# Sparse attention with a gated convolution: last output in 64-row transfers, x without padding, a convolution by shifted ranges

## The chip, the cores and the metric

One of the eight cores of a Trainium2 chip runs the whole program. The metric is the time of one execution in device microseconds (us), lower is better. The host only lays the arrays out.

## The reference

Eight batches of 576 tokens, eight heads of 64 columns. Four heads attend locally, four with a stride of 32; their outputs side by side are x (576 x 512 per batch). Then a causal convolution of five taps per column makes a gate, and a matrix product makes a value:

```python
x = np.ascontiguousarray(attn_out.transpose(0, 2, 1, 3)).reshape(B, S, H * D)
xp = np.concatenate([np.zeros((B, K - 1, D), dtype=np.float32), x], axis=1)
gate_pre = np.zeros((B, S, D), dtype=np.float32)
for k in range(K):
    gate_pre += conv_w[k][None, None, :] * xp[:, k:k + S, :]
gate = 1.0 / (1.0 + np.exp(-gate_pre))
val = x @ w_val
return (gate * val @ w_out).astype(np.float32)
```

## The kernel before

**Tiles.** Every batch is done for its first 512 tokens (MAIN); the last 64 tokens (REST) of all eight batches are gathered in the tile xe and done at the end as a ninth "batch" of 8 x 64 tokens (`b == B`). x lies transposed, columns on the partitions: tiles of 128 partitions x 4 column tiles (index ct or e) x 512 tokens. For float32 accuracy each operand of a product is split in two parts of type fp32r, high and low, and a product is three: high by high, high by low weight, low by high. The parts of x are xhi and xlo, two buffers each, taken in turn by the batches; the parts of the gated value are ghi and glo; the weights are wv and wo, two tiles each.

**Where the operands lie.** Lines 128 to 130 make the parts of x with 16 more elements ahead of each row of 512 (PADX): rows of 528 elements, 2112 bytes apart, and the 512 tokens begin 64 bytes into each. The rows of ghi, glo, wv and wo are 512 elements, 2048 bytes apart, and these tiles follow one another without a gap (lines 132 to 137), so all of their rows begin at the same distance from a multiple of 2048. xe is allocated between the parts of x and ghi.

**Value (line 457) and projection (line 473).** For each batch four chains of twelve matmuls of 512 columns make the value: stationary wv, moving xhi or xlo. VectorE multiplies the result by the gate (GV), ScalarE makes the high part, GpSimd the low part. Four more chains of twelve make 128 rows of output each: stationary ghi or glo, moving wo. In the ninth batch xhi[1] and xlo[1] take the place of ghi and glo (line 455).

**Gate (line 430).** ScalarE and VectorE do the five taps, except for the first two column tiles of batch 0 (CONV, line 541). There TensorE does them: GpSimd builds diagonal matrices in ghi and glo (line 438), and 15 matmuls of 512 columns, five taps by three products, read x at starts 4 to 0 tokens early (line 443). The four elements ahead of each row that they reach are zeroed once by two ScalarE copies (line 516).

**Output (line 496).** ScalarE scales a chain's result into one of two buffers of 128 x 512 (osb, a ring of two) and SyncE's queue (SP) issues one transfer of 128 rows, 256 KB. In the ninth batch the 128 partitions of a chunk are 64 rows of one batch and 64 rows of the next, 576 rows apart; line 495 describes them as one transfer by the destination pattern `[[S * DM, 2], [DM, REST], [1, DM]]`. In the very last chunk, m = 3, ScalarE does one half of the columns and VectorE the other.

**Order.** Each instruction is a step with a number, in the order in which the code adds it; SEQUENCE (line 543) is the order in which the steps are issued, written out by hand, with `f` tokens for filler matmuls. Each engine works its own steps in that order. It ends with "1482 1485 1483 1484 1491 1486 1487 1488 1492 1493 1494 1489 1490": matmul chains of chunks 0, 1, 3, 2 of the ninth batch, and the scaling and the transfer of chunk 3 ahead of those of chunk 2. Chunk 3 takes the output buffer that chunk 1 has had, chunk 2 that of chunk 0. Early in the sequence step 102 is VectorE's subtraction that makes the first third of xlo of batch 0; the GpSimd step before it in the sequence is 61 (low part of wv2) and the one behind it 143 (first scaled probabilities, PS, of the strided heads).

Of the kernel before, what the change touches and what calls it, by code (L numbers as in the profile page):

```python
# [8 lines left out]
F32 = mybir.dt.float32  # L9
F32R = mybir.dt.float32r  # L10
# [11 lines left out]
KC = 5  # L22
PADK = KC - 1
PADX = 16
# [34 lines left out]
def tile_sparse_attention_moe(  # L59
# [22 lines left out]
    def tiles(n, shape, name, dtype=F32, space=None):  # L82
        return [(space or pool).tile(shape, dtype, name=f"{name}{i}") for i in range(n)]
# [42 lines left out]
    vSs = pool.tile([P, 8, 256], F32, name="vSs")  # L126
    xss = tiles(2, [P, 4, PADK + S], "xs")
    xhp = tiles(2, [P, 4, PADX + MAIN], "xhi", F32R)
    xlp = tiles(2, [P, 4, PADX + MAIN], "xlo", F32R)
    xhi, xlo = [t[:, :, PADX:] for t in xhp], [t[:, :, PADX:] for t in xlp]  # L130
    xe = pool.tile([P, 4, B, PADK + REST], F32, name="xe")
# [7 lines left out]
    cws = tiles(2, [P, 4, KC], "cws", F32R)  # L139
    cw64 = pool.tile([P, 4, KC, 2], U32, name="cw64")  # L140
# [167 lines left out]
    def attend_local(b):  # L308
# [3 lines left out]
        for u in range(3):  # L312
# [65 lines left out]
            dve(group, V.tensor_tensor, out=lo, in0=mine, in1=hi.bitcast(F32), op=ALU.subtract)  # L378

# [52 lines left out]
    def gate(b):  # L432
        xs = xss[b % 2]
        for e in range(4):
            gt, group = gates[e][:, :], f"G{b}.{e}"
            if (b, e) in CONV:

                dg = diags[e]
                wide = [P, KC, P]
                for h in range(2):  # L440
                    gps(group, G.affine_select, out=dg[:, h, :, :], in_=cws[h][:, e, :, None].to_broadcast(wide),
                        pattern=[[0, KC], [-1, P]], compare_op=ALU.is_equal, fill=0.0, base=0, channel_multiplier=1)
                cp = m_ps.next()[:, :]
                terms = [(h, xx, k) for k in range(KC)
                         for h, xx in ((0, xhp[b % 2]), (1, xhp[b % 2]), (0, xlp[b % 2]))]
                pe(group, [mm(cp, dg[:, h, k, :], xx[:, e, PADX - PADK + k:PADX - PADK + k + MAIN], i == 0, i == len(terms) - 1)
                           for i, (h, xx, k) in enumerate(terms)])
                act(group, A.activation, out=gt, in_=cp, func=AF.Tanh, scale=0.5)
                continue
# [29 lines left out]
    def project(b):  # L479

        for m in range(4):
# [16 lines left out]
            if b < B:  # L498
                dst = out[b * S + m * P:b * S + m * P + P, :]
            else:  # L500
                first = out[2 * m * S + MAIN:2 * m * S + MAIN + 1, :]
                dst = bass.AP(tensor=first.tensor, offset=first.offset, ap=[[S * DM, 2], [DM, REST], [1, DM]])
            plan.add("sp", group, [(nc.sync.dma_start, dict(out=dst, in_=osb))])
# [12 lines left out]
    for t in (xhp[0], xlp[0]):  # L516
        act("zero xs", A.copy, out=t[:, 0:2, PADX - PADK:PADX], in_=none[:, :, None].to_broadcast([P, 2, PADK]))
# [26 lines left out]
f0x6 f0x4 f0x3 f0x6 44 0 1 32 73 71 37 22 74 72 2 18 3 75 7 46 45 8 5 38 9 33 35 47 181 10 17 11 23 76 48 4 12 21 6 50  # L544
29 20 27 13 56 24 34 81 25 14 49 87 16 31 78 15 39 88 80 103 26 89 62 90 104 f0x1 79 40 91 41 105 119 77 92 187 120
183 51 257 93 121 94 260 52 19 95 57 259 106 96 f0x3 f0x1 f0x1 53 182 258 58 107 54 184 30 55 108 185 122 97 109 28
111 64 63 110 59 99 42 136 123 205 65 98 137 158 f0x3 43 138 186 139 124 140 112 f0x2 60 141 125 113 36 100 114 126
188 127 159 f0x1 101 61 115 142 66 84 102 128 160 143 193 116 129 161 131 210 83 189 130 70 85 132 209 190 82 289 133
144 86 134 67 145 117 272 f0x1 f0x1 191 264 135 118 162 199 192 211 146 273 266 163 69 265 194 164 274 263 147 195 149
275 148 206 196 276 154 277 165 150 68 166 290 306 151 278 197 291 280 421 207 167 155 279 156 423 152 198 307 171 169  # L550
308 200 157 292 153 170 201 168 309 293 176 294 172 202 177 323 310 267 295 178 296 281 173 422 179 174 225 297 324
219 420 180 175 325 282 261 283 220 326 284 226 213 262 311 208 221 212 298 214 327 345 f1x1 301 312 203 222 313 429
# [89 lines left out]
```

## Time and profile before

| | us |
|---|---|
| runs, median of 3 (331.93 to 332.74) | 332.56 |
| the profiled execution, its own time | 329.11 |
| span of the profiled execution, first to last instruction | 327.3 |
| TensorE (PE) busy | 297.6 (91%) |
| VectorE (DVE) busy | 229.0 (70%) |
| ScalarE (ACT) busy | 217.5 (66%) |
| GpSimd (POOL) busy | 149.4 (46%) |

Line 54 is the line of the helper that issues all steps, so most rows carry it; they are told apart by their tiles, written out<-in. PEld is TensorE's loading of stationary operands, which overlaps PE. Matmuls are pipelined, so the distance from one start to the next says more than the duration of one. SPq is the issue of transfers by SyncE. Square brackets at the end of a timeline row give the idle time of the engine before it and what ended it; "x2" means that neighbours of one kind were merged.

### The profile page before, as it was taken

The numbers are of one execution on the slowest core, as the hardware profiler recorded it, in microseconds if no ns is written. First come the engines' busy times: TensorE is split into PE (matmuls) and PEld (weight loads), VectorE is DVE, ScalarE is ACT, GpSimd is POOL, SyncE is SP. The second block draws the span as 40 slices with busy tenths as digits, with TensorE's granted clock in tenths as the row PEclk, the third lists the DMA queues.
The fourth block names the chain that finished last, engine by engine and source line by source line (L and its number), as shares of the span: only waits on it lengthen the run. The fifth ranks groups of instructions, "written<-read, shape, count | busy, mean of one in ns | idle before, by whom it ended". The sixth has DMA issues, their size and how long they took to land.

```text
span 327.3 us, 10519 instructions
## 1 busy us (share of the span) xinstructions
PE 297.6 (91%) x4406; PEld 236.9 (72%) x4409; DVE 229.0 (70%) x435; ACT 217.5 (66%) x499; POOL 149.4 (46%) x202
## 2 busy tenths in 40 slices
PE   8668999999999999999999999999999999999400
PEld 2346778888788888888788888787877887887300
DVE  5878799997789978996668867966945944850000
ACT  7568778975879599786986968888668355342010
POOL 7378666764377437833636453036126134042000
PEclk9979999999999999999999999999999999999955
DMA  7988586477627474742733241320130200100101
GB/s 229 389 299 237 186 268 194 117 239 240 203 87 214 140 218 156 218 149 71 233 120 118 70 153 64 114 93 13 45 102 2 97 32 34 64 32 10 50 28 42
DMA packets 20263, 43.96 MB, mean 134 GB/s; under 512 B 3000, under 2 KB 8888, under 8 KB 19640
## 3 DMA queue, kind: packets, MB, share of 16 engines
q1 hardware_dynamic: 20216, 43.28, 40.5%
q8 instruction: 35, 0.57, 0.8%
q14 instruction: 12, 0.10, 0.1%
HBM read 33.84 MB, written 9.44 MB: 132 GB/s over the span
## 4 chain that ended last, share of the span: by engine, by line
PE 77%; DMA 7%; POOL 4%; ACT 3%; DVE 2%; issue 1%; POOLq 0%; ACTq 0%; SPq 0%; DVEq 0%
PE m_ps L54 55%; PE x_ps L54 10%; PE s_ps L54 8%; PE t_ps L54 4%; DMA out_dram<-osb 3%; DMA qSs<-in_qS_dram 2%; POOL glo L54 2%; DMA osb<-in_w_out_dram 2%; DVE GV L54 1%; ACT ghi L54 1%; POOL xlo L54 1%; ACT BDL L54 1%; ACT xhi L54 1%; PE m_ps L165 1%; DVE gate L54 1%
## 5 line engine op out<-in xcount | busy, mean ns | idle before, releaser
L54 DVE SCALAR_TENSOR_TENSOR gate<-xs,cw,gate 128x512 f32<-128x512 f32 x120 | 91.5, 786 | 8.5 <-ACT gate L54 8.0
L54 PE MATMUL m_ps<-xhi,wv 128*128 128x512 f32 x288 | 91.8, 400 | 0.0
L54 PE MATMUL m_ps<-wo,ghi 128*128 128x512 f32 x256 | 80.4, 395 | 0.0
L54 PEld LDWEIGHTS m_ps<-xhi,wv 128*128 128x128 f32 x288 | 53.0, 188 | 12.3 <-issue 0.4
L54 POOL TENSOR_TENSOR glo<-GV,ghi 128x512 fp32r<-128x512 f32 x32 | 42.2, 1322 | 34.8 <-ACT ghi L54 31.5
L54 PE MATMUL m_ps<-xlo,wv 128*128 128x512 f32 x144 | 56.6, 393 | 0.0
L54 PEld LDWEIGHTS m_ps<-wo,ghi 128*128 128x128 f32 x256 | 47.2, 188 | 9.8
L54 POOL TENSOR_TENSOR PB<-SML,ST 128x256 f32<-128x256 f32 (+1 forms) x48 | 28.2, 603 | 50.5 <-DVE ST L54 42.3
L54 PE MATMUL m_ps<-wo,glo 128*128 128x512 f32 x128 | 50.2, 392 | 0.4 <-POOL glo L54 0.4
L54 DVE SCALAR_TENSOR_TENSOR GV<-gate,m_ps 128x512 f32<-128x512 f32 x36 | 24.4, 681 | 22.2 <-PE m_ps L54 9.3
L54 ACT COPY BDL<-t_ps 32x128 f32<-32x128 f32 (+2 forms) x108 | 34.2, 318 | 4.2 <-PE t_ps L54 2.7
L54 ACT ACTIVATE osb<-m_ps 128x512 f32<-128x512 f32 (+1 forms) x36 | 21.1, 593 | 22.4 <-PE m_ps L54 11.5
L54 DVE TENSOR_TENSOR xlo<-x_ps,xhi 128x256 fp32r<-128x256 f32 (+1 forms) x56 | 24.9, 454 | 15.6 <-ACT xs L54 8.6
L54 ACT COPY BDS<-PT 32x288 f32<-32x288 f32 x64 | 27.6, 432 | 8.6 <-PE x_ps L54 4.2
L54 PEld LDWEIGHTS m_ps<-xlo,wv 128*128 128x128 f32 x144 | 27.1, 188 | 6.2
L54 ACT CAST xhi<-x_ps 128x256 fp32r<-128x256 f32 (+1 forms) x56 | 22.3, 403 | 11.3 <-PE x_ps L54 9.8
L54 PEld LDWEIGHTS m_ps<-wo,glo 128*128 128x128 f32 x128 | 24.0, 188 | 6.5 <-POOL glo L54 1.3
L54 DVE TENSOR_REDUCE ST<-SML 128x6 f32<-128x390 f32 (+1 forms) x45 | 24.2, 546 | 4.4 <-ACT SML L54 3.9
L54 ACT COPY xs<-x_ps 128x288 f32<-128x288 f32 (+1 forms) x53 | 22.2, 430 | 7.6 <-PE x_ps L54 7.4
L54 ACT CAST ghi<-GV 128x512 fp32r<-128x512 f32 x32 | 19.5, 618 | 10.9 <-DVE GV L54 10.7
L54 ACT ACTIVATE gate<-gate 128x512 f32<-128x512 f32 x34 | 21.2, 629 | 8.3 <-DVE gate L54 8.1
L54 POOL TENSOR_TENSOR PS<-SMS,ST 128x256 f32<-128x256 f32 (+1 forms) x32 | 16.3, 523 | 20.3 <-DVE ST L54 20.3
(108 smaller groups left out, 434.0 us busy)
## 6 DMA issues: line engine op xcount, KB each, us to landing
out_dram<-osb SPq DMA_DIRECT2D x36, 256.0 KB, 2.4
vLs<-in_vL_dram SPq DMA_DIRECT2D x8, 640.0 KB, 9.2
qLs<-in_qL_dram SPq DMA_DIRECT2D x16, 288.0 KB, 3.8
KBL<-in_kL_dram SPq DMA_DIRECT2D x16, 288.0 KB, 3.9
KBS<-in_kS_dram SPq DMA_DIRECT2D x16, 288.0 KB, 4.8
qSs<-in_qS_dram SPq DMA_DIRECT2D x16, 288.0 KB, 3.7
vSs<-in_vS_dram SPq DMA_DIRECT2D x32, 128.0 KB, 3.8
raw<-in_w_val_dram SPq DMA_DIRECT2D x2, 512.0 KB, 4.8
```

The source lines that it names most:

```text
L54: fn(**kw)
L165: plan.filler = lambda at: T.matmul(out=at, lhsT=idle[:, :P], rhs=idle[:, :], start=True, stop=True)
```

## The change

Three edits. The ninth batch's chunks leave as two transfers each, of 64 rows (64 partitions of osb). The parts of x lose the 16 elements ahead of each row, and xe moves ahead of xs in the order of allocation, so that the rows of xhi and xlo are 2048 bytes apart and these tiles lie directly ahead of ghi, glo, wv and wo. The two TensorE convolutions of batch 0, which read ahead of the row, now write shifted ranges of the result instead: tap "back" adds x[0:512-back] to columns back to 511. For odd back, range and start are kept even: the large matmul starts one token later, and a second matmul of two columns adds (0, x[0]) from a small new tile, lead, with the same stationary operand. Column 0 of lead is zeroed by two ScalarE copies (in place of the two before); column 1 is filled by two GpSimd copies of x[0], steps 103 and 104. All later steps are numbered two higher; apart from that SEQUENCE is the same, with "103 104" put in right behind step 102.

```diff
-PADX = 16
...
+    xe = pool.tile([P, 4, B, PADK + REST], F32, name="xe")
     xss = tiles(2, [P, 4, PADK + S], "xs")
-    xhp = tiles(2, [P, 4, PADX + MAIN], "xhi", F32R)
-    xlp = tiles(2, [P, 4, PADX + MAIN], "xlo", F32R)
-    xhi, xlo = [t[:, :, PADX:] for t in xhp], [t[:, :, PADX:] for t in xlp]
-    xe = pool.tile([P, 4, B, PADK + REST], F32, name="xe")
+    xhi = tiles(2, [P, 4, MAIN], "xhi", F32R)
+    xlo = tiles(2, [P, 4, MAIN], "xlo", F32R)
...
+    lead = tiles(2, [P, 2, 2], "lead", F32R)
...
             dve(group, V.tensor_tensor, out=lo, in0=mine, in1=hi.bitcast(F32), op=ALU.subtract)
+            if (b, u) == (0, 0):
+                for t, x in zip(lead, (xhi[0], xlo[0])):
+                    gps(group, G.tensor_copy, out=t[:, :, 1], in_=x[:, 0:2, 0])
...
-                terms = [(h, xx, k) for k in range(KC)
-                         for h, xx in ((0, xhp[b % 2]), (1, xhp[b % 2]), (0, xlp[b % 2]))]
-                pe(group, [mm(cp, dg[:, h, k, :], xx[:, e, PADX - PADK + k:PADX - PADK + k + MAIN], i == 0, i == len(terms) - 1)
-                           for i, (h, xx, k) in enumerate(terms)])
+                terms = [(h, xx, back) for back in range(KC)
+                         for h, xx in ((0, xhi[b % 2]), (1, xhi[b % 2]), (0, xlo[b % 2]))]
+                calls = []
+                for h, xx, back in terms:
+                    odd = back % 2
+                    calls.append((cp[:, back + odd:], dg[:, h, PADK - back, :], xx[:, e, odd:MAIN - back]))
+                    if odd:
+                        calls.append((cp[:, back - 1:back + 1], calls[-1][1], lead[xx is xlo[b % 2]][:, e, :]))
+                pe(group, [mm(*c, i == 0, i == len(calls) - 1) for i, c in enumerate(calls)])
...
-                dst = out[b * S + m * P:b * S + m * P + P, :]
+                moves = [(out[b * S + m * P:b * S + m * P + P, :], osb)]
             else:
-                first = out[2 * m * S + MAIN:2 * m * S + MAIN + 1, :]
-                dst = bass.AP(tensor=first.tensor, offset=first.offset, ap=[[S * DM, 2], [DM, REST], [1, DM]])
-            plan.add("sp", group, [(nc.sync.dma_start, dict(out=dst, in_=osb))])
+                moves = [(out[(2 * m + i) * S + MAIN:(2 * m + i + 1) * S, :], osb[i * REST:i * REST + REST]) for i in range(2)]
+            plan.add("sp", group, [(nc.sync.dma_start, dict(out=o, in_=i)) for o, i in moves])
...
-    for t in (xhp[0], xlp[0]):
-        act("zero xs", A.copy, out=t[:, 0:2, PADX - PADK:PADX], in_=none[:, :, None].to_broadcast([P, 2, PADK]))
+    for t in lead:
+        act("zero xs", A.copy, out=t[:, :, 0], in_=none.to_broadcast([P, 2]))
```

## Rows read from the trace of the kernel before

**Rows 1.** The page: the chain that ended last, shares of the span by engine.
```profile
PE 77%; DMA 7%; POOL 4%; ACT 3%; DVE 2%; issue 1%; POOLq 0%; ACTq 0%; SPq 0%; DVEq 0%
```

**Rows 2.** Busy us by stretch: PE, PEld, DVE, ACT, POOL; clock, DMA share, GB/s.
```profile
75.00:150.00 75.00, 75.00 (x1386) 61.80 (x1385) 64.87 (x129) 59.63 (x144) 39.83 (x54) 1.00 0.55 175
```

**Rows 3.** Timeline of the end: last matmuls, scaling and transfers of the ninth batch.
```profile
301.29 0.60 ACT L54 ACTIVATE osb<-m_ps 128x512 f32<-128x512 f32 x1 [2.19 <-PE m_ps L54]
...
306.38 0.39 PE L54 MATMUL m_ps<-wo,xlo 128*128 128x512 f32 x1
...
312.35 0.87 ACT L54 ACTIVATE osb<-m_ps 128x256 f32<-128x256 f32 x2 [10.46 <-DMA out_dram<-osb]
312.77 0.42 DVE L54 TENSOR_SCALAR osb<-m_ps 128x256 f32<-128x256 f32 x1 [16.91 <-ACT osb L54]
313.22 1.12 SPq L54 DMA_DIRECT2D out_dram<-osb  x2
```

**Rows 4.** Stretches as in rows 2: a 128-row output, the end (two), two 64-partition loads.
```profile
289.50:290.40 0.90, 0.90 (x5) 0.73 (x4) 0.90 (x3) 0.73 (x2) 0.00 (x0) 1.00 0.77 291
317.00:325.00 8.00, 0.00 (x0) 0.00 (x0) 0.00 (x0) 0.00 (x0) 0.00 (x0) 0.50 0.13 51
326.00:327.20 1.20, 0.00 (x0) 0.00 (x0) 0.00 (x0) 0.00 (x0) 0.00 (x0) 0.50 0.00 0
164.00:167.00 3.00, 3.00 (x22) 2.43 (x16) 1.04 (x2) 2.23 (x6) 2.50 (x2) 1.00 0.72 234
```

**Rows 5.** SyncE's timeline: a 128-row output, two 64-partition loads; landing of outputs (tile osb).
```profile
276.36 0.33 SPq L54 DMA_DIRECT2D out_dram<-osb  x1
...
162.64 1.18 SPq L54 DMA_DIRECT2D qSs<-in_qS_dram  x2
...
DMA to landing us min/median/max: 2.0/2.4/4.3
```

**Rows 6.** PE timeline: first matmul of a chain and of the next: value, projection, ninth projection.
```profile
258.27 0.63 PE L54 MATMUL m_ps<-xhi,wv 128*128 128x512 f32 x2
...
261.07 0.40 PE L54 MATMUL m_ps<-wo,ghi 128*128 128x512 f32 x1
...
281.00 0.61 PE L54 MATMUL m_ps<-wo,ghi 128*128 128x512 f32 x2
...
283.72 0.40 PE L54 MATMUL m_ps<-xhi,wv 128*128 128x512 f32 x1
...
301.04 0.62 PE L54 MATMUL m_ps<-wo,xhi 128*128 128x512 f32 x2
...
303.82 0.39 PE L54 MATMUL m_ps<-wo,xhi 128*128 128x512 f32 x1
```

**Rows 7.** PE timeline: second TensorE convolution; transposes and what follows; group of weight loads.
```profile
35.73 0.40 PE L54 MATMUL m_ps<-xlo,ghi 128*128 128x512 f32 x1
...
38.50 0.40 PE L54 MATMUL m_ps<-xlo,ghi 128*128 128x512 f32 x1
...
40.66 0.66 PE L54 MATMUL t_ps<-ident,PB 128*128 128x128 f32 x4
41.07 0.47 PE L54 MATMUL m_ps<-xhi,wv 128*128 128x512 f32 x1
...
L54 PEld LDWEIGHTS m_ps<-xhi,ghi 128*128 128x128 f32 x10 | 1.8, 188 | 0.6 <-issue 0.2
```

**Rows 8.** Timeline of batch 0: GpSimd and VectorE around step 102, GpSimd later, TensorE.
```profile
24.50 0.63 POOL L54 TENSOR_TENSOR PS<-SMS,ST 128x256 f32<-128x256 f32 x1
25.03 0.56 DVE L54 TENSOR_TENSOR xlo<-x_ps,xhi 128x384 fp32r<-128x384 f32 x1 [0.61 <-ACT xhi L54]
...
29.67 1.30 POOL L54 TENSOR_TENSOR wo<-w,wo 128x512 fp32r<-128x512 f32 x1 [0.99 <-ACT wo L54]
...
30.82 1.33 ACT L54 COPY BDS<-PT 32x288 f32<-32x288 f32 x3
...
33.36 1.21 PE L54 MATMUL x_ps<-BDS,vSs 128*32 128x72 f32 x64
```

More of the change, by code (lines that the diff above doesn't have):

```diff
@@ L543 @@
 SEQUENCE = """
[L544 to L552, printed above, removed]
[47 rows of a table removed]
+f0x6 f0x4 f0x3 f0x6 44 0 1 32 73 71 37 22 74 72 2 18 3 75 7 46 45 8 5 38 9 33 35 47 183 10 17 11 23 76 48 4 12 21 6 50
+29 20 27 13 56 24 34 81 25 14 49 87 16 31 78 15 39 88 80 105 26 89 62 90 106 f0x1 79 40 91 41 107 121 77 92 189 122
+185 51 259 93 123 94 262 52 19 95 57 261 108 96 f0x3 f0x1 f0x1 53 184 260 58 109 54 186 30 55 110 187 124 97 111 28
+113 64 63 112 59 99 42 138 125 207 65 98 139 160 f0x3 43 140 188 141 126 142 114 f0x2 60 143 127 115 36 100 116 128
+190 129 161 f0x1 101 61 117 144 66 84 102 103 104 130 162 145 195 118 131 163 133 212 83 191 132 70 85 134 211 192 82
+291 135 146 86 136 67 147 119 274 f0x1 f0x1 193 266 137 120 164 201 194 213 148 275 268 165 69 267 196 166 276 265 149
+197 151 277 150 208 198 278 156 279 167 152 68 168 292 308 153 280 199 293 282 423 209 169 157 281 158 425 154 200 309
+173 171 310 202 159 294 155 172 203 170 311 295 178 296 174 204 179 325 312 269 297 180 298 283 175 424 181 176 227
+299 326 221 422 182 177 327 284 263 285 222 328 286 228 215 264 313 210 223 214 300 216 329 347 f1x1 303 314 205 224
[47 rows of a table added]
 """
```

94 rows, old and new, of the table SEQUENCE are left out of this document.

## The prediction

> **What bounds the kernel now.** I read the page's chain of waits first. Over the span of 327.3 us it runs on TensorE for 77%, on transfers for 7%, on no other engine for more than 4% [rows 1]. The busy time by stretch says the same from within: in 75 to 150 us TensorE has no free time that shows, at a clock of 1.00, and VectorE, ScalarE and GpSimd have some [rows 2]. So a us of TensorE's time in the middle is worth most of a us.
>
> The end is another matter. The last matmul starts at 306.38 and takes 0.39 [rows 3]: TensorE is done at 306.8, 20.5 us before the span ends. Read the bracket of the next row: ScalarE stood idle for 10.46 us until a transfer of an output freed its buffer, scaled chunks 3 and 2 from 312.35, and their transfers were issued from 313.22 [rows 3]. The stretches say why: at the end the 16 DMA engines are busy for a share of 0.13, which is 2 of 16, and move 51 GB/s; a stretch that holds an ordinary output of 128 rows has 0.77 and 291 GB/s [rows 4]. The same 256 KB need 5.1 us at 51 GB/s. Four chunks need 20.6, and since there are two output buffers, two chunks queue before ScalarE's wait and two behind it. Data flow until about 326; the stretch from 326.0 to 327.2 has none, so some 1.3 us lie between the last data and the end [rows 4].
>
> **The output, in two transfers.** What the rows of the end have in common and the others lack is an outer dimension of 2 in the destination. I take it that the two engines come from that 2, and that a transfer whose outer dimension is 64 rows spreads wide. The nearest row for 64: the two loads of qSs over 64 partitions, issued from 162.64 [rows 5], run beside a smaller load at 0.72 and 234 GB/s [rows 4]. Their partitions are every second one and not half of the array, and they read HBM, so this is near and not the same.
>
> *The Trainium skill, "DMA: Bandwidth & Descriptors", section "Why a DMA increments its semaphore by 16 and not by 1", says that a transfer uses the largest number of engines up to 16 that divides both patterns' outermost dimension: 2 before, which rows 4 bear out, and 16 after, which no row of an output of 64 rows shows.*
>
> The new end, from rows. A scaling starts 0.09 after the last matmul of its chain (301.29 against a matmul that ends at 301.20) and takes 0.60 [rows 3]. Chunk 1 is issued at 301.9 as before, now twice: an issue takes 0.33 for an output and 0.59 for a load over 64 partitions [rows 5], I take 0.45. It lands 2.0 to 2.4 later [rows 5], at 304.4 to 304.8. Chunk 3 is ready at 304.1 and waits for that buffer; ScalarE's half and VectorE's half take 0.87 from start to issue [rows 3], so its two transfers are issued by 306.6. Chunk 2 is ready at 306.86, needs 0.60, and is issued at 307.48, its second half at 307.9. An ordinary output needs 2.0 from issue to landing and the end 1.3 beyond the last data; landing and end overlap, so I take 3.0 from the last issue: 310.9. That is **16.4 us** less than 327.3. Bounds: with issues of 0.33 and the smaller transfers a half us quicker 310.3 (17.0 less); with the slowest landing of any output, 4.3 [rows 5], 313.2 (14.1 less). Nothing late stands behind it: TensorE's end at 306.8 and chunk 2's fixed latencies become the bound.
>
> **x without padding.** Between one chain's first matmul and the next one's lie twelve matmuls: 2.80 us in this value chain, 2.72 in a projection, 2.78 in a projection of the ninth batch [rows 6]. The last two tell most: the same moving wo, the same clock, and only the stationary operand comes from the padded xhi in place of ghi. Value chains without a break are of two kinds in about equal numbers, this one and one that takes 2.78 like the ninth projection. I take the distance of the rows, 2112 bytes against 2048, for the cause; after the change all these operands' rows begin at equal distances from a multiple of 2048, as ghi's and wo's do now. Then 36 value chains save 0.07 each, 2.5 us, the four last projections 0.24, and the 30 convolution matmuls (12 steps in 2.77 [rows 7], 231 ns each against 227) 0.1: 2.9 on TensorE. TensorE carries about 85% of the chain outside start and end [rows 1], so **2.4 us** of it reach the end. Bounds: nothing, if another cause sets the pace, and 2.9; a pace that turns worse I exclude up to what the slowest rows show, 2.80 a chain, another 0.4.
>
> **Convolution by shifted ranges.** Per convolution two odd taps by three products give six more pairs of a weight load and a matmul of two columns, twelve in all; the large matmuls lose at most 4 of 512 columns, under 0.05 us together. The load for the small matmul can hide under the large one before it. The load behind it, I assume, can start only once the small matmul has begun, so the array waits. The nearest row: four transposes, each with a load of 128 columns, start 0.41 us before what follows, 103 ns a pair [rows 7]. I take 0.11 a pair: **1.3 us**, at TensorE's pace, all on its path. Bounds: nothing, if loads overtake fully, and 188 ns, a whole load [rows 7], 2.3 us.
>
> **Two copies on GpSimd.** Steps 103 and 104 sit in its queue behind wv2 and ahead of the probabilities that start at 24.50; they must wait for VectorE's xlo, done at 25.59 [rows 8]. So PS starts at 25.6 plus two tiny copies, some 0.4 us, 1.5 us late, with everything behind it: the second diagonals, PS, wv3. Who waits: VectorE's transposes of PS, ScalarE's BDS, whose last copy ends at 32.15, and TensorE's x_ps at 33.36 [rows 8]. That is 1.2 of slack, and the first convolution, 0.65 longer, adds to it. GpSimd itself was idle for 0.99 before 29.67 [rows 8] and regains most there. I take **0.2 us**; bounds nothing and 1.5. The two ScalarE copies that zero lead take the place of two before: nothing, ScalarE has that work either way.
>
> **Sum.** -16.4 - 2.4 + 1.3 + 0.2 = -17.3 us, made against the profiled execution (span 327.3, own time 329.11, so 311.8). The median of the runs lies 3.45 above that execution's time; I carry the difference over: 332.56 - 17.3 = **315.3 us**.
>
> **Rivals.** *The pace of the value chains has another cause* and stays: 2.4 us less gain, 317.7. For it: 5 ns a matmul is little, and reads of x differ in more than the distance of rows. Against it: the ninth projections, which alone among projections touch padded tiles and alone are slow. 0.28.
>
> *64 rows get only a few engines*, say 4: 102 GB/s, 2.6 us a chunk. Chunk 3's scaling then waits for chunk 1 until 305.8, its data run to 310.0, those of chunk 2 to 312.6, the end comes at 313.9: 318.3. No row shows such a transfer; the 234 GB/s of loads over 64 partitions speak against it. 0.07.
>
> *The limit belongs to these rows or to halves of the partitions, not to the outer 2.* Then the bytes still move at 51 GB/s, the 20.6 us stay, the extra issues add 0.5, the convolution 1.3 and GpSimd 0.2; without a gain from x that is 334.6, with all of it 332.2. It decides from the point where a pair of transfers is no faster than 51 GB/s and x gives under 1 us. Against it: nothing but the outer 2 sets these transfers apart from the ordinary ones in size, source or row length; for it: no output of 64 rows was seen. 0.05, of which 0.03 end slower.
>
> *The Trainium skill speaks for this rival: "SBUF — State Buffer", section "Can I just issue two DMAs to hit both halves?", says that transfers on the two halves of the partitions serialize and that one transfer over all 128 partitions is the way to reach all ports. The trace disagrees with its use here: the single transfer over 128 partitions is the one that moves at 51 GB/s.*
>
> **How the numbers follow.** The forecast, both gains there, has 0.60: 315.3, and with its terms' bounds 312.5 to 317. The second case at 317.7 and the third at 318.3 carry the range up to 318.8; what is left out is the rest of the third and the fourth. Low: the end's 17.0, x's 2.9, a convolution for 0.3 and no loss on GpSimd give 313; the runs' own spread of 0.8 takes it to 312.5. A measurement of this kernel tells 0.3%, 1.0 us, from no change. Faster by more: 0.95; within: 0.02; slower: 0.03.
>
> **What would show it.** In the new profile the end should have a short burst with a share of the 16 engines several times 0.13, ScalarE without the wait of 10.46, and a span that ends 4 us after the last matmul; value chains should take 2.72; each convolution some 0.65 longer than its 3.5; PS on GpSimd behind the copies, after 25.6. A share of 0.13 at the end would make the prediction wrong outright, value chains at 2.78 to 2.80 by 2.4 us.

## The result, and the profile after

The changed kernel takes 315.15 us in the median of 4 runs (313.18 to 315.54) and the kernel before 332.25 beside it (330.23 to 332.74): a ratio of 0.9485, with a 95% interval from 0.9427 to 0.9542. That is 17.1 us less; 17.3 were predicted. The profiled execution took 315.54 with a span of 313.5. It isn't laid straight beside the profile of before: that was one of its kernel's quicker executions (329.11), this one of its kernel's slower, and it has a stall of its own (below). So stretches are compared rather than spans.

The chain of waits still runs on TensorE, and transfers fell from 7% to 4% of it [rows 1]:

```profile
PE 78%; ACT 6%; DVE 4%; DMA 4%; POOL 3%; issue 2%; SPq 1%; POOLq 0%; DVEq 0%; ACTq 0%
```

The timeline of the end, as [rows 3]:

```profile
303.67 0.60 ACT L53 ACTIVATE osb<-m_ps 128x512 f32<-128x512 f32 x1 [2.18 <-PE m_ps L53]
...
307.29 0.38 ACT L53 ACTIVATE osb<-m_ps 128x256 f32<-128x256 f32 x1 [3.02 <-DMA out_dram<-osb]
...
308.63 0.39 PE L53 MATMUL m_ps<-wo,xlo 128*128 128x512 f32 x1
309.06 0.60 ACT L53 ACTIVATE osb<-m_ps 128x512 f32<-128x512 f32 x1 [1.39 <-PE m_ps L53]
...
309.68 0.47 SPq L53 DMA_DIRECT2D out_dram<-osb  x1
```

The wait of 10.46 has become 3.02, and it costs nothing: ScalarE scales its half of chunk 3 at 307.29 and is done well before the last chain ends at 309.02 (308.63 + 0.39). The last scaling now waits for TensorE, not for a buffer. The last instruction of all starts at 313.45, 4.43 us after the last matmul; before it was 20.45. (The span ends 0.05 us later, in both.)

The stretches of the end, with the columns of [rows 4]: the pair of the second chunk, the pairs of the last two, and what is left.

```profile
305.40:306.90 1.50, 1.50 (x8) 1.23 (x8) 0.00 (x0) 0.00 (x0) 0.00 (x0) 1.00 0.79 175
309.30:312.10 2.80, 0.00 (x0) 0.00 (x0) 0.00 (x0) 0.35 (x1) 0.00 (x0) 1.00 0.83 184
312.20:313.40 1.20, 0.00 (x0) 0.00 (x0) 0.00 (x0) 0.00 (x0) 0.00 (x0) 0.64 0.00 0
```

The share is 0.79 to 0.83 against 0.13 and the rate 175 to 184 GB/s against 51. It is still not the 291 of an ordinary output: a chunk's 256 KB need about 1.45 us.

Two value chains of the new kernel, as [rows 6]: the first matmul of one and of the next.

```profile
289.08 0.62 PE L53 MATMUL m_ps<-xhi,wv 128*128 128x512 f32 x2
...
291.80 0.62 PE L53 MATMUL m_ps<-xhi,wv 128*128 128x512 f32 x2
```

That is 2.72 where it was 2.80, and the matmuls within are 226 to 228 ns apart. The chains of the ninth projection take 2.72 too.

The first convolution's start and successor, then the second's with two of its six small matmuls, and the first value chain, as [rows 7]:

```profile
29.98 0.81 PE L53 MATMUL m_ps<-xhi,glo 128*128 128x512 f32 x2
...
34.78 1.21 PE L53 MATMUL x_ps<-BDS,vSs 128*32 128x72 f32 x64
...
36.57 0.73 PE L53 MATMUL m_ps<-xhi,ghi 128*128 128x512 f32 x2
...
37.61 0.17 PE L53 MATMUL m_ps<-lead,ghi 128*128 128x2 f32 x1
37.64 0.47 PE L53 MATMUL m_ps<-xhi,ghi 128*128 128x510 f32 x1
37.95 0.17 PE L53 MATMUL m_ps<-lead,ghi 128*128 128x2 f32 x1
...
40.89 1.21 PE L53 MATMUL x_ps<-BDS,vSs 128*32 128x72 f32 x64
...
43.03 0.71 PE L53 MATMUL m_ps<-xhi,wv 128*128 128x512 f32 x2
```

From its first matmul to the next operation the second takes 4.32 (36.57 to 40.89), in the trace of before 3.78: 0.54 for six pairs, 90 ns each. From one small matmul to the next are 0.34 (37.61 to 37.95), where a large one alone has some 0.23. The first convolution takes 4.80, 0.48 more than the second.

That 0.48 has its cause on GpSimd and VectorE, as [rows 8]:

```profile
25.69 0.49 DVE L53 TENSOR_TENSOR xlo<-x_ps,xhi 128x384 fp32r<-128x384 f32 x1
...
26.25 0.19 POOL L53 CAST lead<-xlo 128x2 fp32r<-128x2 f32 x1 [0.22 <-DVE xlo L53]
26.39 0.63 POOL L53 TENSOR_TENSOR PS<-SMS,ST 128x256 f32<-128x256 f32 x1
...
29.39 0.71 DVE L53 STREAM_TRANSPOSE PT<-PS 128x512 f32<-128x512 f32 x1 [0.87 <-POOL PS L53]
30.02 0.85 DVE L53 TENSOR_TENSOR xlo<-x_ps,xhi 128x256 fp32r<-128x256 f32 x2
```

The probabilities start at 26.39 in place of 24.50, VectorE's transpose waits 0.87 us for them, and the two steps that make the rest of xlo stand behind it and end at 30.87. The convolution had begun at 29.98 and needs them.

Last, a stall that the prediction has no step for, in TensorE's timeline:

```profile
51.65 1.18 PE L53 MATMUL x_ps<-BDL,vLs 128*32 128x96 f32 x42 [0.26 <-DMA vLs<-in_vL_dram]
53.97 0.28 PE L53 MATMUL x_ps<-BDL,vLs 128*32 128x96 f32 x3 [1.15 <-issue]
```

TensorE stands still for 1.15 us in the middle of a group, with nothing shown that it waits for.

A table of times within the traces, in us, is used throughout. "Start to value" runs from the first matmul of the first convolution to the first value matmul, "next 48" from there to the 49th value matmul, "pace" from there to the end of the last matmul, "end" from there to the start of the last instruction of all, 0.05 us before the end of the span.

| kernel | start to value | next 48 | pace | end |
|---|---|---|---|---|
| before | 11.49 | 35.27 | 230.42 | 20.45 |
| changed | 13.05 | 36.99 | 229.00 | 4.43 |
| the same again | 12.65 | 35.16 | 228.79 | 4.43 |
| the two transfers alone | 11.47 | 37.81 | 230.32 | 4.46 |
| changed, outputs as before | 12.87 | 35.26 | 228.94 | 20.51 |
| changed, padded | 13.10 | 35.35 | 230.37 | 4.43 |
| changed, 64 bytes of skew | 12.92 | 35.18 | 230.56 | 4.46 |
| changed, no small matmuls | 11.47 | 37.65 | 228.81 | 4.43 |

What lies ahead of the first convolution is not in the table. It takes 29.58 us before, 29.98 in the changed kernel and 31.43 in the same again, and 28.45 to 32.25 over all eleven traces. TensorE's granted clock is part of that: in ten of the traces it falls to 0.50, the lower of its two levels, for 3.4 or 6.8 us in all before the first convolution, and not in the same place. Here is one stretch, first in the trace of the changed kernel, then in that of the same again:

```profile
27.60:31.00 3.40, 3.09 (x84) 2.48 (x85) 2.53 (x5) 2.63 (x8) 3.40 (x5) 1.00 0.93 289
27.60:31.00 3.40, 3.40 (x80) 3.27 (x72) 2.20 (x4) 2.19 (x7) 3.40 (x5) 0.50 0.93 293
```

### The profile page after: what moved, and what is told of

It is laid out like the page before. It is cut to its first block, busy times and chain, and to the rows that moved or that the text cites. A ratio compares the mean times of both kernels' runs of the same rounds, so it can differ in the third digit from the quotient of the medians.

```text
span 313.5 us, 10550 instructions
## 1 busy us (share of the span) xinstructions
PE 298.1 (95%) x4418; PEld 238.4 (76%) x4421; DVE 230.7 (74%) x435; ACT 217.6 (69%) x499; POOL 149.9 (48%) x204
## 4 chain that ended last, share of the span: by engine, by line
PE 78%; ACT 6%; DVE 4%; DMA 4%; POOL 3%; issue 2%; SPq 1%; POOLq 0%; DVEq 0%; ACTq 0%
PE m_ps L53 58%; PE x_ps L53 11%; PE s_ps L53 7%; PE t_ps L53 3%; DMA vLs<-in_vL_dram 2%; DMA KBL<-in_kL_dram 2%; POOL glo L53 2%; DVE gate L53 1%; ACT BDL L53 1%; ACT xhi L53 1%; DVE GV L53 1%; SPq L53 1%; POOL xlo L53 1%; ACT gate L53 1%; ACT ghi L53 1%
## 5 line engine op out<-in xcount | busy, mean ns | idle before, releaser
L53 PE MATMUL m_ps<-xhi,wv 128*128 128x512 f32 x288 | 90.5, 396 | 0.0
```

What stands on the lines that cost most here:

```text
L53: fn(**kw)
```

## The experiments

**The two transfers alone.** The kernel before, with this edit:

```diff
-            plan.add("sp", group, [(nc.sync.dma_start, dict(out=dst, in_=osb))])
+            plan.add("sp", group, [(nc.sync.dma_start, dict(out=o, in_=i)) for o, i in moves])
```

> The kernel before with the two 64-row transfers and nothing else of the change. Theory (the outer dimension of 2 held the end to two engines): the end loses its 10.46 us wait, the span ends 4 to 4.6 us after the last matmul as in the changed kernel, the time is 332.3 - 16 = 316 us (315 to 317.5), and the value chains stay at 2.78 to 2.80 us. Rival (a good part of the gain came from the placement of x): 319 us or more.

313.68 us (312.93 to 316.08), ratio 0.9451 (0.9389 to 0.9512), so below the 315 to 317.5 expected. ScalarE's wait for a buffer is gone here too:

```profile
307.48 0.39 ACT L54 ACTIVATE osb<-m_ps 128x256 f32<-128x256 f32 x1 [3.02 <-DMA out_dram<-osb]
```

The end is 4.46, the value chains stay at 2.78 to 2.80 and the convolutions at 3.75 and 3.78. The split alone brings all of what can be measured.

**The same, the other way round.** The changed kernel with the ninth batch's output as one transfer again, the edit above reversed:

> The changed kernel with the ninth batch's outputs as the kernel before has them, one transfer a chunk with an outer dimension of 2; x without padding and the convolution by shifted ranges stay. Theory (the split alone carries the gain, the other two parts cancel at the path's end to within 1 us): the end is again some 20.4 us after the last matmul with a share of 0.13, ScalarE waits 10 us or more for a buffer, the value chains stay at 2.72, and the time is 330 to 332. Rival (the other two parts gain what the prediction gave them, 1.1 us and more, and lone runs hid it): 329 to 330.5, and TensorE's last matmul ends more than 1 us earlier than the 306.8 of the kernel before, counted from the first value chain.

329.94 us (328.95 to 331.69), ratio 0.9989 (0.9947 to 1.0032) to the kernel before, which holds no change as well as 1.7 us less. Its timeline and a stretch of its end:

```profile
312.36 0.87 ACT L53 ACTIVATE osb<-m_ps 128x256 f32<-128x256 f32 x2 [10.40 <-DMA out_dram<-osb]
```

```profile
317.00:325.00 8.00, 0.00 (x0) 0.00 (x0) 0.00 (x0) 0.00 (x0) 0.00 (x0) 0.50 0.13 50
```

The share of 0.13 and the wait are back. This trace has no stall, like that of before, so the two can be set side by side: the first value matmul starts at 42.50 against 41.07, 1.43 later, of which 1.38 arise after the first convolution's start; the stretch from the 49th value matmul takes 1.48 less; the last matmul ends at 306.70 against 306.76. What x without padding gains, the convolution gives back. In the trace the theory's account closes. The time decides nothing: 329.94 lies in the rival's 329 to 330.5 and just under the theory's 330 to 332, the ratio stands for 0.4 us, and its interval holds both. The sign named for the rival, a last matmul more than 1 us earlier counted from the first value chain, is there as well (1.49), but x's gain alone brings it, so it doesn't tell the two apart.

**Padding put back, all else as changed.**

```diff
-    xhi = tiles(2, [P, 4, MAIN], "xhi", F32R)
+    xhi = [t[:, :, 16:] for t in tiles(2, [P, 4, 16 + MAIN], "xhi", F32R)]
```

and the same for xlo.

> The changed kernel, with 16 elements ahead of each row of xhi and xlo again (rows 2112 bytes apart); convolution by shifted ranges and split output stay. Theory (the placement of x sets the pace of the value chains): twelve matmuls of a value chain take 2.78 to 2.80 us again in place of 2.72, the ninth projections 2.78, and the time is 315.2 + 2.4 = 317.6 us. Rival (something else in the change sped the chains up): chains stay at 2.72, 315.2 us.

315.02 us (314.88 to 317.78), ratio 0.9519 (0.9455 to 0.9583): not to be told from the changed kernel by its time, and 2.6 less than the 317.6 expected. The value chains are back at 2.78 to 2.80 and the pace at 230.37: 1.4 to 1.6 us more than the unpadded kernels.

**64 unused bytes between xlo and ghi.** x stays unpadded, its rows 2048 bytes apart, but everything behind it, wv and wo too, begins 64 bytes further on.

```diff
+    skew = pool.tile([P, 16], F32, name="skew")
     ghi = pool.tile([P, 4, MAIN], F32R, name="ghi")
```

> The changed kernel with 64 unused bytes per partition between xlo and ghi: rows of x still 2048 bytes apart, but no longer at the same distance from a multiple of 2048 as those of wv and wo. Theory A (the distance of the rows sets the pace): twelve matmuls of a value chain stay at 2.72 us. Theory B (the two operands' common distance from a multiple of 2048 does): value chains and the ninth projections go back towards 2.75 to 2.80, the other projections stay at 2.72, and the way from the 49th value matmul to the last matmul goes from 229 back to 230.3 us.

315.51 us (314.68 to 316.43), ratio 0.9521 (0.9449 to 0.9593). The pace is 230.56, as with padding. TensorE's timeline of its value chains, the start of a chain, the matmuls three steps on, and the start of the next chain:

```profile
287.75 0.63 PE L53 MATMUL m_ps<-xhi,wv 128*128 128x512 f32 x2
...
288.45 0.63 PE L53 MATMUL m_ps<-xhi,wv 128*128 128x512 f32 x2
...
290.55 0.63 PE L53 MATMUL m_ps<-xhi,wv 128*128 128x512 f32 x2
```

Three matmuls take 0.70, a chain of twelve 2.80. The distance of the rows is 2048 as in the fast kernel; what differs is where x's rows and wv's rows lie against each other. The projections, whose ghi and wo moved together, keep 2.72; the ninth ones, which read xhi and xlo, take 2.75. That is theory B: the quick pace belongs to operands whose rows begin at the same distance from a multiple of 2048 bytes. That 2048 is the period is not shown: only this one shift of 64 bytes and the padded rows were tried, and a multiple of a smaller number would fit them as well.

**Without the small matmuls.** The twelve matmuls of two columns are left out, so what the first token adds to columns 1 and 3 is left out too.

```diff
-                    if odd:
-                        calls.append((cp[:, back - 1:back + 1], calls[-1][1], lead[xx is xlo[b % 2]][:, e, :]))
```

> The changed kernel without the twelve matmuls of two columns (what they add to the first four tokens of the first two column tiles of batch 0 is left out). Theory (each pair holds TensorE up by about 90 ns): the second convolution goes from 4.32 us between its first matmul and the next work to about 3.75, the first from 4.80 to about 4.2, the time is 315.2 - 1.1 = 314.1 us. Rival (the array waits there for other things, data or code): the convolutions keep 4.3 us and more, 315.2 us.

314.51 us (313.55 to 316.62), ratio 0.9492 (0.9429 to 0.9556). The convolutions take 3.76 and 3.78 again, and from the first of them to the first value chain 11.47, though GpSimd's copies are still there. The pairs are the cost of the second convolution. The first is shorter than the 4.2 expected because GpSimd's lateness reached nothing here, and that is not for want of the pairs. The convolution's first matmul and the work behind the convolution, and VectorE's last steps for xlo:

```profile
32.17 0.82 PE L53 MATMUL m_ps<-xhi,glo 128*128 128x512 f32 x2
...
35.93 1.21 PE L53 MATMUL x_ps<-BDS,vSs 128*32 128x72 f32 x64
```

```profile
30.84 0.85 DVE L53 TENSOR_TENSOR xlo<-x_ps,xhi 128x256 fp32r<-128x256 f32 x2
```

TensorE came to the convolution at 32.17, behind a stretch at the clock of 0.50, when xlo had been done since 31.69. Over the seven traces with both the pairs and the copies it is the same: the first convolution takes 0.29 to 0.48 longer than the second in the five in which it begins at 28.45 to 30.01, and 0.07 in the two in which it begins at 31.43 and 32.25.

**The same again,** unaltered, to learn what a repeat moves:

> The changed kernel, unaltered, profiled again. Theory (TensorE's stalls between 51 and 54 us in its first profile, behind a load of vLs and then behind nothing that shows, come and go with the order in which transfers land): the new profile has them elsewhere, smaller or not at all, and the value chain that began at 56.4 begins at 54.5 to 55.5; span 311 to 313. Rival (the change itself causes them): stalls of the same 1.4 us in the same place, span 313.5.

313.88 us (312.62 to 314.55), ratio 0.946 (0.9405 to 0.9516); span 312.5, no stall between 51 and 54. So the change doesn't bring the stall with it every time; the two transfers alone, without the rest of the change, have one too.

**One transfer with another outer dimension.** The ninth batch is laid out token by token, not batch by batch, so that a chunk is 16 tokens of 8 batches and leaves as one transfer over 128 rows whose outer dimension is 16. Core of the edit (the gate's and the parts' views change in the same way):

```diff
-                moves = [(out[(2 * m + i) * S + MAIN:(2 * m + i + 1) * S, :], osb[i * REST:i * REST + REST]) for i in range(2)]
+                first = out[MAIN + 16 * m:MAIN + 16 * m + 1, :]
+                moves = [(bass.AP(tensor=first.tensor, offset=first.offset, ap=[[DM, 16], [S * DM, B], [1, DM]]), osb)]
```

> The changed kernel with the ninth batch's tokens in another order, token by token and batch by batch within a token, so that the 128 partitions of a chunk are 16 tokens of 8 batches; each chunk leaves as one transfer whose destination pattern is 16 x 8 rows, outermost 16. The output is the same. Theory (the engines follow the outermost dimension; packets of 64 neighbouring partitions are slow because half of the partitions share half of the ports): all 128 partitions again, packets of 2 KB take 85 ns in place of 154, a chunk's data 0.85 us, one issue; the span ends 3.2 to 3.5 us after the last matmul in place of 4.43, ScalarE's wait of 3.0 for chunk 1 falls below 2.3: 313.4 us, if writing every eighth element of a row costs nothing on the path. Rival (rows that lie 576 apart are slow to write): 51 GB/s or packets of 154 ns again, the end 4.4 us or more after the last matmul.

319.9 us (318.64 to 321.6), ratio 0.9653 (0.9599 to 0.9707). The stretches of its last two chunks:

```profile
315.60:316.80 1.20, 0.00 (x0) 0.00 (x0) 0.00 (x0) 0.26 (x1) 0.00 (x0) 1.00 0.78 205
317.10:318.30 1.20, 0.00 (x0) 0.00 (x0) 0.00 (x0) 0.00 (x0) 0.00 (x0) 0.70 0.79 210
```

One transfer with an outer 16 has a share of 0.78 as the pairs have; the count of transfers isn't what counts. The end took 4.48 all the same, where the theory had 3.2 to 3.5: packets take 84 ns, as it expected, but a chunk's data need 1.27 us and not 0.85, and a transfer lands 2.8 us after its issue where an ordinary output needs 2.4 [rows 5]. Why is open. The 5 us that the run loses to the changed kernel lie ahead of the end, in the group of the ninth batch's gates, here and in the changed kernel:

```profile
L53 DVE SCALAR_TENSOR_TENSOR gate<-xe,cw,gate x16: 1135/1222/1296, 278.5 to 299.0; 128x512 f32<-128x512 f32 x16
```

```profile
L53 DVE SCALAR_TENSOR_TENSOR gate<-xe,cw,gate x16: 742/744/752, 278.3 to 292.7; 128x512 f32<-128x512 f32 x16
```

The new layout makes these write every eighth element, and one takes 1222 ns and not 744. VectorE now holds TensorE up: the chain of waits has its gates for 23.1% from 290 to 320, and the last matmul of the value chains starts at 303.2 where the changed kernel has 297.0. A part of this is the clock. TensorE stood still for 3.16 us until 296.27, and soon after the granted clock fell to 0.50, the lower level:

```profile
296.27 0.72 PE L53 MATMUL m_ps<-xhi,wv 128*128 128x512 f32 x2 [3.16 <-ACT osb L53]
```

```profile
297.10:300.50 3.40, 3.40 (x10) 2.63 (x9) 3.07 (x4) 1.51 (x3) 0.69 (x1) 0.50 0.19 73
```

The two value chains from 296.27 on took 7.17 us, the same two in the changed kernel 5.44, so the clock's share is some 1.7 us. The next run has such a stretch as well (297.6 to 301.0).

**Two transfers from every second partition.** The same layout, each chunk as osb[0::2] and osb[1::2].

> As the run with one transfer, but each chunk leaves as two transfers of 64 rows, from every second partition. Theory (neighbouring partitions 0 to 63 reach half of the ports): packets take 85 ns, a pair's data 0.9 us after each other, the span ends 3.9 to 4.1 us after the last matmul. Rival (the smaller transfers, or two of them at once, are slow for another reason): packets of 154 ns, 4.4 us.

321.93 us (319.74 to 323.03), ratio 0.9703 (0.9635 to 0.9772). This was to tell what makes the packets of 2 KB slow: in the changed kernel one takes 154 ns, in an ordinary output 85. From every second partition they take 84 to 91, so the slow packets belong to 64 neighbouring partitions. But the end isn't quicker for it:

```profile
316.90:319.60 2.70, 0.00 (x0) 0.00 (x0) 0.00 (x0) 0.20 (x1) 0.00 (x0) 1.00 0.66 187
```

187 GB/s, a share of 0.66 only, and an end of 4.49: with quick packets the engines are idle for longer between them. The rival's 4.4 is nearer than the theory's 3.9 to 4.1, though its packets of 154 ns are not there.

*The Trainium skill, "SBUF — State Buffer", section "Can I just issue two DMAs to hit both halves?", says that transfers on the two halves run on the same 16 engines and one after the other. A pair's 1.45 us, against 0.9 for the ordinary output of [rows 4], are in line with that but don't show it: the single transfer over all 128 partitions in the run before takes 1.27 us for as many rows. Its advice of one transfer over 128 partitions is the slowest of all here when that transfer has an outer dimension of 2, at 50 to 51 GB/s.*

**Additions for the small matmuls, and two queues.** The changed kernel, where GpSimd adds the first token's parts and multiplies by the odd taps, VectorE adds the products to columns 1 and 3, and ScalarE's queue issues the second transfer of the last pair.

```diff
-                    if odd:
-                        calls.append((cp[:, back - 1:back + 1], calls[-1][1], lead[xx is xlo[b % 2]][:, e, :]))
...
+                dve(group, V.tensor_tensor, out=cp[:, 1:4:2], in0=cp[:, 1:4:2], in1=fix[:, e, :], op=ALU.add)
...
+            if (b, m) == (B, 2):
+                o, i = moves.pop()
+                plan.add("act", group, [(nc.scalar.dma_start, dict(out=o, in_=i))])
```

> The changed kernel with two edits. The twelve two-column matmuls give way to additions: GpSimd adds the first token's two parts and multiplies by the two odd taps (three instructions on 2 elements a row in place of the two copies), and VectorE adds the two products of each convolution to columns 1 and 3 of its result before the Tanh. And of the last pair of output transfers ScalarE's queue issues the second, right behind its scaling, beside SyncE's first. Theory (each pair costs TensorE 90 ns, and the second issue of a pair stands 0.5 us behind the first on the way to the end): both convolutions are back at 3.75 to 3.78 us from their first matmul to the next chain, 1.1 us less; the span ends 3.9 to 4.1 us after the last matmul in place of 4.43 to 4.46; together 1.5 us, about 312.5 beside 313.9 to 315.2 of the changed kernel. Rival 1 (the pair's data set the end, 1.4 us for 262 KB however they are issued, since both halves share the same engines): the end stays at 4.3 or above and the time gains 1.1 at most. Rival 2 (VectorE's addition stands in its queue behind a convolution that is not done, and holds back what is behind it): the convolutions are short again, but the first value chains start no earlier than in the changed kernel, and the time stays.

314.9 us (310.86 to 315.73), ratio 0.943 (0.9369 to 0.9491). Its timeline holds both effects:

```profile
36.39 0.73 PE L53 MATMUL m_ps<-xhi,ghi 128*128 128x512 f32 x2
...
40.17 1.21 PE L53 MATMUL x_ps<-BDS,vSs 128*32 128x72 f32 x64
...
53.60 0.84 PE L53 MATMUL s_ps<-KBL,qLs 128*32 128x128 f32 x18 [1.72 <-issue]
...
309.94 0.56 ACTq L53 DMA_DIRECT2D out_dram<-osb  x1
```

The second convolution is back at 3.78 (36.39 to 40.17), the first is at 4.55 because it still waits 0.51 us for xlo, behind GpSimd's three instructions; the span ends 4.08 us after the last matmul. Rival 1 falls, by 0.35 us at the end. The time, though, can't be told from the changed kernel's 315.15: the interval is 4 us wide, and this trace too has stalls. It is no version that is shown to be better.

## Why the prediction was right

**The end** is the gain, as predicted: 16.0 us (20.45 less 4.43) against 16.4. Its cause is shown from both sides: the split alone brings it, taking the split back takes it away, and an outer dimension of 16 in a single transfer does what 64 does. The size was off by 0.4 at the tail: the span ends 4.48 us after the last matmul and not 4.1. The issue of the second half came 1.18 after the last matmul (309.02 to 310.20; 1.13 predicted), but from there to the end of the span it was 3.30 and not 3.0: I had priced the landing by an ordinary output, and a pair moves 175 to 184 GB/s, not 291. The buffer for chunk 3 came free 3.0 us after the second chunk's first issue, where I had 2.5 to 2.9; the last chain covered that.

**x without padding** gained what the chains said, 2.72 for 2.80, and 2.72 for 2.78 in the ninth projection. The cause was named half right. The prediction took "the distance of the rows, 2112 bytes against 2048"; the kernel with the skew has 2048 and is slow. The second half of that sentence, equal distances from a multiple of 2048, is what held, with the period not shown. The size was too large: 2.4 predicted, 1.4 to 1.6 measured from the 49th value matmul on; before that, between the first and the 49th, the traces without a stall differ by 0.1 (35.27 and 35.16 to 35.26). The term that was too large is the 36 value chains at 0.07 each. Only 22 of them run without a break: these went from 2.55 (14 of them) or 2.58 (eight) between their first and their last start to 2.49, some 1.46 in all. Twelve begin behind other work; these took 2.63 to 2.68 before and take 2.61 to 2.67 now, 0.02 less in the mean, and two more are broken in the middle. Of the four last projections two gained, 0.06 each, and the 30 convolution matmuls gained nothing (3.76 and 3.78 without the pairs, 3.78 and 3.78 before). From the 49th value matmul on these gains add up to some 1.8 on TensorE, of which 1.4 to 1.6 reach the end.

**The convolution** cost 90 ns a pair against 110, 1.1 us for twelve against 1.3, and **GpSimd's copies** 0.48 in the profiled execution and 0.07 in the repeat (4.39 against 4.32), against 0.2. They cost this only where TensorE is at the first convolution before xlo is done. The route is the one predicted, over VectorE's transpose, but it ends in a place that I had not named: not in x_ps at the end of the convolution but in xlo at its beginning. Together 1.16 in the repeat and 1.38 to 1.61 in the other traces of the table with pairs before the first value chain, predicted 1.5.

**The sum** was right partly by luck: x gained 0.9 less than I had, the end 0.4 less, and the account from traces is -16.0 - 1.5 + 1.4 = -16.1. The medians say 17.1. The 1.0 between them lies within the spread of the runs, about 2.5 us for either kernel, and no run here assigns it: the account holds neither the start, which differs by 1.45 us between two traces of the changed kernel, nor the stalls.

Of the rivals, the second (few engines for 64 rows) and the third (rows or halves set the limit) are out by the share of 0.79 to 0.83, the first by the chains at 2.72; the padded kernel is the first rival made real, and its time can't be told from the forecast's.

## What to carry to other kernels

When a short transfer at the end of a kernel is slow, look at the DMA share before the bytes: 0.13 is 2 engines of 16, and the outermost dimension of the pattern is the place to look. Look for a layout that gives a large outermost dimension without costing another engine anything; a view that writes every eighth element cost more here than the transfer could return. And set the operands of long chains of matmuls at a common distance from a multiple of 2048 bytes, by their pace in the trace (whether a smaller number than 2048 does is not shown here), but count the gain only for the chains that run without a break.

## What was not expected of the hardware

- Matmuls of 128 by 512 started every 226 to 228 ns where both operands' rows began at the same distance from a multiple of 2048 bytes, and some 233 ns apart in the mean of a value chain (226 to 236 one by one) where it did not: with 64 bytes between them and rows 2048 bytes apart, and with x's rows 2112 bytes apart.
- A matmul of two columns between large ones cost 90 ns with its load of 128 columns (188 ns), half of a whole load.
- A packet of 2 KB took 154 ns in transfers from 64 neighbouring partitions and 84 to 91 in those from 128 or from every second one, yet pairs of either kind needed about 1.4 us.
- In five of the eleven traces (changed, the two transfers alone, no small matmuls, one transfer with an outer 16, additions) the stretch "next 48" is 1.7 to 2.9 us longer than the 35.2 to 35.4 of the others. In each of them TensorE stands still once or twice in 50 to 61 us, for 1.2 to 2.0 us the longest time, with "issue" as the only reason that the timeline names. Its cause wasn't tried and stays open. The traces hold a candidate: each of the six stalls ends 2.2 to 2.6 us after a packet of 16 KB on the instruction queue starts (51.73 and 53.97 in the changed kernel), and that packet comes 1.8 us or more later behind the one before it than the same packet does in any of the six traces without a stall. That is a coincidence in time, and no run tests it. The stall is larger than all that x and the convolution moved, and with the differing starts it may be why medians don't tell those apart.
